# Sums of log decays in four 64x64 tiles, by exchanging the token halves of every second batch

## The chip, the cores and the metric

The kernel runs on one core of a Trainium2 chip. The metric is the device time of one execution, in microseconds. Most single executions of one and the same kernel here lie within about 1% of their median (the farthest, in e10, 1.6% below it, apart from one of 1174.87 us named below), so differences of less than 1% are read from repeated runs or from the trace, not from one time. The state of a one-core run ("fast" or "slow") is told only by its distance from the fastest run of its kernel: a run over 1.5% above it is left out of the ratio. Where that matters (above all in e10) the text says so.

## The reference

Two stages: a recurrence over 768 tokens for 4 batches of 8 heads, with a 40x40 state for each, and a two-layer perceptron on its output.

```python
# r, k, v, w, a, b: (4, 8, 768, 40) float32; w is the decay, between 0.85 and 0.95
for t in range(S):
    y[:, :, t] = einsum('bhd,bhde->bhe', rt, state)
    Sa = einsum('bhde,bhe->bhd', state, at)
    state_decay = state * wt[:, :, None, :] - einsum('bhd,bhe->bhde', Sa, bt)
    state = state_decay + einsum('bhd,bhe->bhde', vt, kt)
x = y.transpose(0, 2, 1, 3).reshape(B * S, H * D)      # 3072 x 320
h = x @ w_in                                           # 320 -> 2048
out = (0.5 * h * (1 + erf(h / sqrt(2)))) @ w_out       # 2048 -> 320
```

## The kernel before

The recurrence is computed in 12 chunks of C = 64 tokens, everything in float32. The kernel keeps two batches on the two halves of the 128 partitions: partition half e holds the 64 tokens of batch 2e+g, and g (0 or 1) is an index along the free dimension. A "pair" in the prediction below is one value of g. P is 128, HP 64, D 40, H 8, G 2, NP 4, DM 320.

Within a chunk, decays multiply up, so their logarithms are summed over the tokens before. That is a matrix product with a triangular mask. The mask `cum_m` is 128x128 and has two triangles on its diagonal and zeros elsewhere, because the two halves are different batches:

```python
def rows_of(src, c, e):
    return src[G * e:G * (e + 1), :, c * C:(c + 1) * C, :].rearrange("g h t d -> t (g h) d")

def fetch(c, n, src, eng, t=None):            # loads of w, b, k: two DMAs for each
    ...
    for e in range(2):
        eng.dma_start(out=t[half(e)].rearrange("p g h d -> p (g h) d")[:, :, :D], in_=rows_of(src, c, e))

def load_VR(c):                               # the load of v by tokens: two DMAs
    VR = turned_in.setdefault(c, {})["VR"] = VR_ring()
    for e in range(2):
        nc.sync.dma_start(out=VR[half(e)].rearrange(...)[:, :, :D], in_=rows_of(v, c, e))

def sums(c):
    logw = raws.pop((c, "w"))
    cum = duo("cum")[:, :, :DM]
    for g in range(G):
        mm(cum[:, g], cum_m, logw[:, g * DM:(g + 1) * DM])          # 128x128, 320 columns
    pt = duo("wT_ps")...
    for n in range(G * NP):                                         # the same sums, transposed
        for x in range(2):
            for e in range(2):
                mm(pt[half(x), e, n], logw[half(e), at:at + HP], cum_m[half(e), half(e)])
    ...                                                             # exponentials: part, wpT, en
```

The other products of the recurrence run in 64x64 or smaller tiles, several at once (in the profile of the kernel before, the 64 records of a QY group, 263 ns each in the mean, fit in a slot of 1.47 us). Apart from the transposes of the state (tn_ps), only these sums use the whole array.

Each chunk also needs the inverse of a triangular 64x64 matrix per head. GpSimd inverts its 32x32 diagonal blocks (tile W). They go to a scratch area in DRAM (`inv`) and come back in another layout (`Tt`). VectorE transposes them (`L`), and TensorE computes the off-diagonal block (products `J`). All DMAs but a few of the last chunk are issued, in order, by one queue, SyncE's. This is the loop, with the calls that the argument touches kept:

```python
for c in range(2, NCH):
    n, n2 = c + 1, c + 2
    corner(c)                     # J: needs L
    make_X(c)
    fill()                        # one piece of the perceptron of an earlier chunk
    load_next(n2)                 # SyncE issues the loads of w, a, b, k, r
    joined(c)
    ...
    make_QY(c)
    outputs(c)
    fill()
    make_A(n)
    load_VR(n2)                   # SyncE issues the load of v
    sums(n2)                      # cum, wT_ps
    turn_state()                  # tn_ps
    ...
    store_inverse(n)              # SyncE: inv <- W, behind the load of v
    fetch_inverse(n)              # SyncE: Tt <- inv, waits for the store
    make_av(n)
    ...
    make_N(n2)                    # SyncE: N to DRAM and back, for GpSimd
    turn_corner(n)                # VectorE: L <- Tt
    ...
```

So the fetch of the inverse for a chunk stands in SyncE's queue behind the load of v for the chunk after it. Dense work of the perceptron (ph and po) fills TensorE's time between the products.

## Time and profile before

| | before |
|---|---|
| median of the first three runs | 758.54 us (758.03 to 761.15) |
| span of the profiled run | 756.8 us |
| TensorE busy | 690.4 us, 91% |
| one chunk in the steady part | 53.05 us, TensorE busy throughout |

The page of the kernel before has a line for the chain that ended last (shares of the span by engine). In the views PE is TensorE, DVE VectorE, ACT ScalarE and POOL GpSimd; SPq is the queue of SyncE that issues DMAs:

```profile
PE 78%; DVE 5%; POOL 5%; issue 5%; SPq 4%; DMA 3%; ACT 1%; POOLq 0%; DVEq 0%; ACTq 0%
```

TensorE carries the chain. The SPq and DMA shares, 7% together, are the ones to compare later. From about 190 us on, TensorE's slices are full, so any slot that leaves TensorE's queue should shorten the span. The prediction below shows these lines.

### The profile page before, as it was taken

The numbers are of one execution on the slowest core, as the hardware profiler recorded it, in microseconds if no ns is written. First come the engines' busy times: TensorE is split into PE (matmuls) and PEld (weight loads), VectorE is DVE, ScalarE is ACT, GpSimd is POOL, SyncE is SP. The second block draws the span as 40 slices with busy tenths as digits, with TensorE's granted clock in tenths as the row PEclk, the third lists the DMA queues.
The fourth block names the chain that finished last, engine by engine and source line by source line (L and its number), as shares of the span: only waits on it lengthen the run. The fifth ranks groups of instructions, "written<-read, shape, count | busy, mean of one in ns | idle before, by whom it ended". The sixth has DMA issues, their size and how long they took to land.

```text
span 756.8 us, 30335 instructions
## 1 busy us (share of the span) xinstructions
PE 690.4 (91%) x13664; PEld 550.9 (73%) x13664; DVE 320.8 (42%) x452; ACT 209.1 (28%) x254; POOL 317.6 (42%) x778
## 2 busy tenths in 40 slices
PE   7456886884999999999999999999999999999997
PEld 4346775652887887887877877878878878778684
DVE  2777438874244345155244353443352552211000
ACT  5124363241232222330341331322223303102020
POOL 3385146850381471570750842833814806500000
PEclk9655798986999999999999999999999999999999
DMA  9797666095763754755845746648547441110100
GB/s 120 131 173 139 120 188 113 20 165 117 134 119 68 144 111 80 135 106 99 145 86 110 133 90 126 125 82 150 106 82 138 102 78 37 34 36 3 31 5 17
DMA packets 302153, 75.68 MB, mean 100 GB/s; under 512 B 290408, under 2 KB 295304, under 8 KB 302024
## 3 DMA queue, kind: packets, MB, share of 16 engines
q1 hardware_dynamic: 301824, 73.58, 51.5%
q8 instruction: 107, 1.75, 1.0%
q14 instruction: 22, 0.18, 0.1%
q10 hardware_dynamic: 200, 0.16, 0.1%
HBM read 59.54 MB, written 10.22 MB: 92 GB/s over the span
## 4 chain that ended last, share of the span: by engine, by line
PE 78%; DVE 5%; POOL 5%; issue 5%; SPq 4%; DMA 3%; ACT 1%; POOLq 0%; DVEq 0%; ACTq 0%
PE po L823 27%; PE ph L815 26%; PE QY L100 5%; PE J L100 2%; PE sap L100 2%; PE cum L100 2%; PE saT_ps L100 2%; PE N_ps L100 2%; PE M_ps L100 2%; DVE W L629 2%; PE av L100 2%; DVE tmp L627 1%; POOL tmp L627 1%; POOL W L629 1%; PE X L100 1%
## 5 line engine op out<-in xcount | busy, mean ns | idle before, releaser
L823 PE MATMUL po<-w_out_sb,gt 128*128 128x320 f32 x768 | 224.5, 445 | 17.4 <-DVE w_out_sb L299 15.5
L815 PE MATMUL ph<-xt,w_in_sb 64*128 64x256 f32 x1920 | 222.8, 385 | 5.9 <-POOL w_in_sb L304 5.5
L815 PEld LDWEIGHTS ph<-xt,w_in_sb 64*128 64x128 f32 x1920 | 183.9, 189 | 30.3 <-POOL w_in_sb L304 6.3
L823 PEld LDWEIGHTS po<-w_out_sb,gt 128*128 128x128 f32 x768 | 143.9, 193 | 80.5 <-DVE w_out_sb L299 21.0
L627 POOL TENSOR_TENSOR tmp<-W,Nb 128x126 f32<-128x126 f32 (+22 forms) x310 | 113.1, 365 | 157.5 <-DMA Nb<-N 133.9
L629 POOL TENSOR_TENSOR W<-W,tmp 128x126 f32<-128x126 f32 (+22 forms) x310 | 118.2, 381 | 24.3
L817 ACT ACTIVATE gt<-ph 128x1024 f32<-128x1024 f32 x48 | 49.2, 1025 | 166.4 <-PE ph L815 166.3
L827 DVE COPY os<-po 128x320 f32<-128x320 f32 x24 | 11.8, 492 | 90.1 <-PE po L823 90.1
L533 DVE TENSOR_TENSOR SM<-M_ps,upper 128x1024 f32<-128x1024 f32 x12 | 14.7, 1224 | 58.8 <-PE M_ps L100 58.8
L694 DVE COPY Tt<-J 32x512 f32<-32x512 f32 x12 | 8.3, 689 | 66.0 <-ACT Tt L694 66.0
L453 POOL TENSOR_TENSOR ks<-k_raw,part 128x640 f32<-128x640 f32 x10 | 21.2, 2123 | 34.6 <-DMA k_raw<-in_k_dram 17.5
L678 ACT COPY Js<-J 128x256 f32<-128x256 f32 x12 | 4.5, 372 | 107.7 <-PE J L100 107.7
L617 POOL MEMSET W<- 128x512 f32 x10 | 5.3, 530 | 68.8 <-DMA inv<-W 68.8
L772 DVE TENSOR_TENSOR xt<-QY,wpT 128x512 f32<-128x512 f32 x24 | 15.5, 686 | 42.2 <-PE QY L100 42.2
L291 ACT ACTIVATE conv<-conv,rebias 128x320 uint32<-128x320 uint32 (+1 forms) x26 | 16.0, 622 | 46.4 <-DVE conv L290 46.4
L817 ACT ACT_TABLE_LOAD x10 | 12.8, 1283 | 42.4 <-PE ph L815 42.4
L533 DVE TENSOR_TENSOR A<-A_ps,upper 128x1024 f32<-128x1024 f32 x12 | 14.7, 1221 | 22.8 <-PE A_ps L100 22.8
L721 DVE COPY SM<-sap 128x640 f32<-128x640 f32 x12 | 9.9, 824 | 30.3 <-PE sap L100 30.1
L533 DVE TENSOR_TENSOR N<-N_ps,upper 128x1024 f32<-128x1024 f32 x12 | 14.7, 1225 | 18.5 <-PE N_ps L100 18.5
L100 PEld LDWEIGHTS QY<-SM,nb 64*64 64x64 f32 x768 | 18.7, 140 | 5.2 <-issue 3.6
L100 PE MATMUL QY<-SM,nb 64*64 64x104 f32 x768 | 21.3, 263 | 1.3 <-DVE SM L533 1.3
L100 PEld LDWEIGHTS av<-VR,A 64*64 64x64 f32 x768 | 13.9, 149 | 11.1 <-DVE A L533 6.3
(159 smaller groups left out, 899.5 us busy)
## 6 DMA issues: line engine op xcount, KB each, us to landing
Nb<-N SPq DMA_DIRECT2D x22, 256.0 KB
VR<-in_v_dram SPq DMA_DIRECT2D x24, 160.0 KB
out_dram<-os SPq DMA_DIRECT2D x48, 80.0 KB
w_tile<-in_w_dram SPq DMA_DIRECT2D x22, 160.0 KB
b_raw<-in_b_dram SPq DMA_DIRECT2D x22, 160.0 KB
k_raw<-in_k_dram SPq DMA_DIRECT2D x22, 160.0 KB
w_out_sb<-in_moe_w_out_dram SPq DMA_DIRECT2D x11, 320.0 KB
N<-N SPq DMA_DIRECT2D x48, 64.0 KB
```

What stands on the lines that cost most here:

```text
L100: nc.tensor.matmul(o, lhsT, rhs, start=first, stop=True, skip_group_check=True)
L291: nc.scalar.activation(power, power, ACT.Relu, bias=rebias, scale=8.0)
L453: eng.tensor_tensor(ks[:, :, :, :D], raws.pop((c, "k")), rwv, ALU.mult)
L533: nc.vector.tensor_tensor(to, pt, upper.unsqueeze(1).to_broadcast([P, 2 * G * NP, C]), ALU.mult)
L627: eng.tensor_tensor(t, W[:, :rows, j:j + 1].to_broadcast([P, rows, rest]), Nb[:, j:j + 1, j + 1:].to_broadcast([P, rows, rest]), ALU.mult)
L629: eng.tensor_tensor(W[:, :rows, j + 1:], W[:, :rows, j + 1:], t, ALU.add)
L721: nc.vector.tensor_copy(SM.rearrange("p g q (a x) c -> p x (g q a) c", x=2)[:, :, :, :D], sap.rearrange("p x g q a d -> p x (g q a) d"))
L772: nc.vector.tensor_tensor(xt[:, :NP, g * P:(g + 1) * P].rearrange("p i (e t) -> p i e t", e=2), Y, wp[:, g, :, :, :C], ALU.mult)
L815: nc.tensor.matmul(ph[:, x, s], w_in_sb[half(x), kt, p * P:(p + 1) * P], xt[half(x), kt], start=kt == 0, stop=kt == NK - 1)
L817: nc.scalar.activation(gt[:, 4 * q:4 * q + 4].rearrange("p (x s) t -> p x s t", x=2), ph, ACT.Gelu)
L823: nc.tensor.matmul(po[:, g], gt[:, f, g * P:(g + 1) * P], w_out_sb[:, f], start=f == 0, stop=f == NF - 1)
L827: nc.vector.tensor_copy(os, po[:, g])
```

## The change

Half of each 128x128 product for the sums is multiplication with zeros. Four products of 64x64 (2 halves by 2 values of g) do the same work without the zeros, but in the old layout all four would fall on the two diagonal tiles of the array (e12 below runs that: a chunk took 52.7 to 52.8 us). The change puts batch 2e+1 on the other half of the partitions (g = 1 exchanged), from chunk 4 on. Then the output of g = 1 goes from half e to half 1-e, and the four products occupy all four tiles (the slot of the sums was 0.54 us, against 1.27 before).

The price: the two values of g of one load now lie on different halves, and the change cuts each load of b, k and v in two by g (w stays whole, since its halves are exchanged by the sums themselves). Two copies out of PSUM are cut in four, because av and sap now put g = 1 in the other bank (no run here tried them without that). TensorE's tile order changes in several products. This is the core of the diff:

```diff
+    def tokens(c, e, g):
+        return half(e ^ g if c >= NB else e)
+    def bank(c, x, g):
+        return x ^ g if c >= NB else x
+    def rows_of_one(src, c, e, g):
+        return src[G * e + g, :, c * C:(c + 1) * C, :].rearrange("h t d -> t h d")
...
     def fetch(c, n, src, eng, t=None):
         for e in range(2):
-            eng.dma_start(out=t[half(e)]..., in_=rows_of(src, c, e))
+            if n == "w" or c < NB:
+                eng.dma_start(out=t[half(e)]..., in_=rows_of(src, c, e))
+                continue
+            for g in range(G):
+                eng.dma_start(out=t[tokens(c, e, g), g], in_=rows_of_one(src, c, e, g))
...                                   # load_VR: cut in the same way
     def sums(c):
-        for g in range(G):
-            mm(cum[:, g], cum_m, logw[:, g * DM:(g + 1) * DM])
+        if c < NB:
+            ...                       # as before
+        else:
+            for g in range(G):
+                for e in range(2):
+                    mm(cum[tokens(c, e, g), g], cum_m[half(e), half(e)], logw[half(e), g * DM:(g + 1) * DM])
...
     def make_av(c):
-            mm(av[half(e ^ x), x, g, i], t["A"][half(e), x, g, i], t["VR"][half(e), g, q, m, :D])
+            mm(av[half(e ^ x), bank(c, x, g), g, i], t["A"][tokens(c, e, g), x, g, i], t["VR"][tokens(c, e, g), g, q, m, :D])
-        nc.scalar.copy(avs[:, :, :DM], av.rearrange("p x g i d -> p x (g i d)"))
+        for g in range(G):            # c >= NB
+            for x in range(2):
+                nc.scalar.copy(avs[:, x, :DM].rearrange("p (g n) -> p g n", g=G)[:, g],
+                               av[:, bank(c, x, g), g].rearrange("p i d -> p (i d)"))
...                                   # make_sa: the same with SM; A, RV, M, QY: other tiles
```

More of the change, by code (lines that the diff above doesn't have):

```diff
@@ L145, in fetch @@
         for e in range(2):
-            eng.dma_start(out=t[half(e)].rearrange("p g h d -> p (g h) d")[:, :, :D], in_=rows_of(src, c, e))
+            if n == "w" or c < NB:
+                eng.dma_start(out=t[half(e)].rearrange("p g h d -> p (g h) d")[:, :, :D], in_=rows_of(src, c, e))
+                continue
+            for g in range(G):
+                eng.dma_start(out=t[tokens(c, e, g), g], in_=rows_of_one(src, c, e, g))
         raws[c, n] = t
@@ L192, in load_VR @@
         for e in range(2):
-            nc.sync.dma_start(out=VR[half(e)].rearrange("p g q m d -> p (g q m) d")[:, :, :D], in_=rows_of(v, c, e))
+            if c < NB:
+                nc.sync.dma_start(out=VR[half(e)].rearrange("p g q m d -> p (g q m) d")[:, :, :D], in_=rows_of(v, c, e))
+                continue
+            for g in range(G):
+                nc.sync.dma_start(out=VR[tokens(c, e, g), g].rearrange("p q m d -> p (q m) d")[:, :, :D],
+                                  in_=rows_of_one(v, c, e, g))
     def load_v(c):
@@ L394, in sums @@
         cum = duo("cum")[:, :, :DM]
-        for g in range(G):
-            mm(cum[:, g], cum_m, logw[:, g * DM:(g + 1) * DM])
+        if c < NB:
+            for g in range(G):
+                mm(cum[:, g], cum_m, logw[:, g * DM:(g + 1) * DM])
+        else:
+            for g in range(G):
+                for e in range(2):
+                    mm(cum[tokens(c, e, g), g], cum_m[half(e), half(e)], logw[half(e), g * DM:(g + 1) * DM])
         pt = duo("wT_ps").rearrange("p e (n t) -> p e n t", t=C)
@@ L533, in masked, with products @@
         nc.vector.tensor_tensor(to, pt, upper.unsqueeze(1).to_broadcast([P, 2 * G * NP, C]), ALU.mult)
-    def products(name, lT, rT, swap):
+    def products(name, lT, rT, swap, c=0):
         pt = duo(name).rearrange("p j (g n t) -> p j g n t", g=G, n=NP)
@@ L541, in products @@
                     for j in range(2):
-                        mm(pt[half(e ^ j if swap else e), j, g, n], lT[half(j, D), g, n, e],
+                        mm(pt[half(e ^ j) if swap else tokens(c, e, g), j, g, n], lT[half(j, D), g, n, e],
                            rT[half(j, D), g, n, e])
@@ L575, in make_RV @@
         t = turned_in[c]
-        t["RV_ps"] = products("RV_ps", t["vT"], t["rT"], False)
+        t["RV_ps"] = products("RV_ps", t["vT"], t["rT"], c >= NB)
         if mask:
@@ L586, in make_A @@
         t["A"] = work.tile([P, 2, G, NP, C], FP32, tag="nT", name="A")
-        t["A_ps"] = products("A_ps", t["kT"], t["aT"], False)
+        t["A_ps"] = products("A_ps", t["kT"], t["aT"], False, c)
         if mask:
@@ L598, in make_av @@
         for g, i, x, e, q, m in units():
-            mm(av[half(e ^ x), x, g, i], t["A"][half(e), x, g, i], t["VR"][half(e), g, q, m, :D])
+            mm(av[half(e ^ x), bank(c, x, g), g, i], t["A"][tokens(c, e, g), x, g, i], t["VR"][tokens(c, e, g), g, q, m, :D])
         avs = t["avs"] = avs_ring()
-        nc.scalar.copy(avs[:, :, :DM], av.rearrange("p x g i d -> p x (g i d)"))
+        if c < NB:
+            nc.scalar.copy(avs[:, :, :DM], av.rearrange("p x g i d -> p x (g i d)"))
+            return
+        for g in range(G):
+            for x in range(2):
+                nc.scalar.copy(avs[:, x, :DM].rearrange("p (g n) -> p g n", g=G)[:, g],
+                               av[:, bank(c, x, g), g].rearrange("p i d -> p (i d)"))
     inverses = {}
@@ L718, in make_sa @@
             at = (g * NP + i) * D
-            mm(sap[half(e), x, g, q, i % NA], Tt[half(e ^ x), x, g, i], xs[half(e ^ x), x, at:at + D])
+            mm(sap[tokens(c, e, g), bank(c, x, g), g, q, i % NA], Tt[half(e ^ x), x, g, i], xs[half(e ^ x), x, at:at + D])
         SM = t["SM"] = SM_ring()
-        nc.vector.tensor_copy(SM.rearrange("p g q (a x) c -> p x (g q a) c", x=2)[:, :, :, :D],
-                              sap.rearrange("p x g q a d -> p x (g q a) d"))
+        to = SM.rearrange("p g q (a x) c -> p x (g q a) c", x=2)[:, :, :, :D]
+        if c < NB:
+            nc.vector.tensor_copy(to, sap.rearrange("p x g q a d -> p x (g q a) d"))
+            return
+        for g in range(G):
+            for x in range(2):
+                nc.vector.tensor_copy(to[:, x, g * NP:(g + 1) * NP],
+                                      sap[:, bank(c, x, g), g].rearrange("p q a d -> p (q a) d"))
     def make_saT(c):
@@ L738, in make_M @@
         t = turned_in[c]
-        masked(flat(t["SM"])[:, :, D:], products("M_ps", t["saT"], t["rT"], False))
+        masked(flat(t["SM"])[:, :, D:], products("M_ps", t["saT"], t["rT"], c >= NB))
     def make_y2(c):
@@ L759, in make_QY @@
             for g, i, x, e, q, m in units():
-                mm(t["QY"][g][half(x), e, i], l_[half(e), g, head_of(i, x)], r_[half(e), g, q, m],
+                mm(t["QY"][g][half(x), e, i], l_[tokens(c, e, g), g, head_of(i, x)], r_[tokens(c, e, g), g, q, m],
                    state[0] is None and n == 0 and i == 0)
```

## The prediction

> **What bounds the kernel now.** I read the page first (busy shares, the 40 slices, the chain), then the busy time of the engines in seven equal stretches, then TensorE's timeline through one chunk, then the waits of TensorE and of the DMA-issuing queue.
>
> From the page, the slices of TensorE and of its granted clock:
>
> ```profile
> PE   7456886884999999999999999999999999999997
> PEclk9655798986999999999999999999999999999999
> ```
>
> The reader is to see two stages. For about a quarter of the span (to about 190 us) TensorE has gaps and the clock varies: loading and converting of the weights and the first chunks. From there on every slice is full and the clock is full. All the changed work lies in the second stage: chunks 4 to 11 are prepared two chunks ahead, by the loop that serves chunks 2 to 9.
>
> The view of stretches, cut at the start of the product that follows the sums in each chunk (columns: length, TensorE busy with instructions, clock, DMA share, GB/s):
>
> ```profile
> 230.68:283.73 53.05, 53.05 (x1134) 1.00 0.60 112
> 283.73:336.78 53.05, 53.05 (x1134) 1.00 0.60 111
> ...
> 548.98:602.03 53.05, 53.05 (x1133) 1.00 0.58 112
> ```
>
> Each chunk takes 53.05 us to the second decimal, and TensorE is busy for all of it. Asked for TensorE's waits between 230 and 654 us, the trace lists none. So here the time is the sum of TensorE's slots: what leaves its queue leaves the span, unless some other engine becomes late.
>
> The timeline of TensorE around the sums of one chunk (start, length, group):
>
> ```profile
> 489.06 4.57 PE L823 MATMUL po<-w_out_sb,gt 128*128 128x320 f32 x16
> 493.57 1.16 PE L100 MATMUL A_ps<-aT,en 40*64 40x64 f32 x64
> 494.66 1.34 PE L100 MATMUL cum<-w_tile,cum_m 128*128 128x320 f32 x4
> 495.93 1.16 PE L100 MATMUL wT_ps<-cum_m,w_tile 64*64 64x64 f32 x64
> 497.02 1.09 PE L418 MATMUL tn_ps<-ident,st 128*128 128x128 f32 x8
> ```
>
> Groups overlap at their edges, so I measure a slot from start to next start. The sums (cum) take 494.66 to 495.93, 1.27 us, on the full 128x128 array, between two groups in 64x64 tiles. The four records are two matmuls, each in two passes for float32.
>
> [...] The group QY<-SM,nb has 64 passes of 64x104 and the slot 1.47 us (486.05 to 487.52); a pass of 320 columns costs 4.5/16 = 281 ns in the po groups, so one of 104 columns some 90 ns, and 64 of them would take 5.8 us one after another: four run at once. And 32-matmul groups of about the same size have a slot of 0.98 us when the next group is in 64x64 too (QY<-rT, 479.50 to 480.49) and 1.07 to 1.10 when it is not (A_ps, N_ps, RV_ps, wT_ps): about 0.1 us for a switch. [...] by these two rows and two others (ScalarE 128x256 372 ns, VectorE 128x320 492 ns):
>
> ```profile
> L721 DVE COPY SM<-sap 128x640 f32<-128x640 f32 x12 | 9.9, 824 | 30.3 <-PE sap L100 30.1
> L601 ACT COPY avs<-av 128x640 f32<-128x640 f32 x12 | 8.3, 691 | 45.9 <-PE av L100 45.9
> ```
>
> Per column that is (691-372)/384 = 0.83 ns on ScalarE and (824-492)/320 = 1.04 ns on VectorE, and about 160 ns fixed on both.
>
> **The change part by part**, for each of eight chunks. The comparison of the instruction order shows nothing else: no group moves, only six groups change their shape or count.
>
> 1. Sums. Two matmuls 128x128 by 320 become four in the four 64x64 tiles: half of the work of the old ones was with the zero blocks of the mask. Each tile has two passes of 320 columns, 2 x 281 = 562 ns, and all four run beside each other with some 15 ns of issue between them (64 records in 0.96 us for sap). Slot about 0.6 us against 1.27: **-0.67 us**.
> 2. No more switch from A_ps into the sums: A_ps's slot of 1.09 should fall towards 1.0: **-0.08 us**. The switch after the sums was part of the 1.27; the one after wT_ps stays.
> 3. Order of tiles. With halves exchanged for the second pair, av and sap visit the tiles as a b c d d c b a, and QY at distances 3 and 5 rather than 4, so a tile is sometimes asked twice running. The group saT_ps has such an order already (a b b a) and its slot (1.13) is only some 0.04 above groups with a regular order. For four groups I take **+0.1 us** in all. RV, M and A only permute tiles in a regular order: 0.
> 4. Copies in four. ScalarE: 4 x (160 + 160 x 0.83) = 1,170 ns for 691, +0.48 us; VectorE: 4 x (160 + 160 x 1.04) = 1,305 for 824, +0.48 us. ScalarE then idles 11.0 us before its next copy, and the sum that reads avs comes 12 us later. VectorE idles 5.6 us before the mask of M_ps, the next thing TensorE needs from it. The buffers of four PSUM slots come round later than that. On the path: 0.
> 5. Loads. Of b, k and v, two DMAs of 64x16x40 become four of 64x8x40: same bytes, same 160-byte rows, six issues more. The same shape took 634 ns an issue in the start (r, four of them); the issues now take about 0.66 us for v. So the queue gets 6 x 0.64 = 3.8 us more per chunk, if nothing is absorbed.
>
> Sum on TensorE: -0.67 - 0.08 + 0.1 = **-0.65 us per chunk, eight times: -5.2 us**, period 52.4 us.
>
> **The rivals.** (a) The DMA-issuing queue becomes the bound. This is the only one I take seriously. Its waits in a chunk:
>
> ```profile
> SPq L651 <- DMA inv<-W: 3.7, 1, 3.7
> SPq L619 <- DMA N<-N: 1.6, 1, 1.6
> SPq L146 <- POOL tmp L627: 0.7, 1, 0.7
> SPq L780 <- DVE st L795: 0.6, 1, 0.6
> SPq L570 <- DVE L L664: 0.5, 1, 0.5
> ```
>
> That is all between 283 and 336 us: the first two are round trips through DRAM on its own path, and only 1.8 us are free. Other chunks have up to 8 us free, about 5 on average. Adding 3.8 us brings the queue close to TensorE's 52.4 us. What is late then is the fetch of the inverse (Tt), which stands behind the added v loads: issued 10.6 to 12.4 us after the sums start, landed some 4 us later, transposed at +16.6, and TensorE needs the result at +19.8 (corner products J). So about 2 us of lateness are free after the shift of 0.65 us. The v loads alone add 1.3 us; those of b and k (2.6) meet a wait of 0 to 3 us on a VectorE transpose[...]. So I expect small stalls in one to three chunks, **+0.4 us in all**; if nothing is absorbed and each chunk loses 1.5 us, the gain is gone (760). (b) The four tiles don't overlap on such wide matmuls, or the two passes block each other: eight passes of 281 ns, 2.2 us, would cost 8 x 1 us and give 766. QY speaks against it at 104 columns. (c) VectorE or ScalarE becomes late: 43% and 28% busy in these chunks, against. (d) Nothing is gained since the sums hide: against, TensorE has no gap that could hide them.
>
> **The range and the chances.** 758.5 - 5.2 + 0.4 gives **753.7 us**. If the sums take 0.8 us and stalls 1.5 us: 757; if the switch saves twice what I took and the tile order costs nothing: 751.8. So 751.8 to 757.2, eight times in ten. A change of 2% is 15 us, three times the whole gain, and neither rival (a) nor (b) reaches it: faster by over 2% 0.01, within 2% 0.975, slower by over 2% 0.015.
>
> **What would show it.** In the changed profile: the slot of cum about 0.6 us, that of A_ps about 1.0; the chunk period 52.4 us with TensorE still busy throughout; slots of sap, av and QY longer by under 0.05 us each; four copies of about 290 and 330 ns with the same next starts; the queue's free waits per chunk reduced by 2 to 4 us. Wrong it would be if TensorE showed waits in J (on the transpose L) in most chunks, if the period changed from chunk to chunk, or if cum's slot stayed above 1 us.

## The result

| | before | changed |
|---|---|---|
| median, runs of the same rounds | 758.28 us (755.59 to 761.15, 6 runs) | 767.11 us (760.32 to 770.52, 6 runs) |
| profiled run: span | 756.8 us | 765.0 us |
| profiled run: mean granted clock of TensorE | 0.936 | 0.926 |

The ratio is 1.0105, with a 95% interval from 1.0059 to 1.0152. Ratios here and below are the mean time of one kernel's fast runs over that of the other's fast runs of the same rounds, so they are not quite the ratio of the medians. The change loses 1%. That is within 2%, but the time lies 10 us above the range of the prediction, on the other side of zero.

**What went as intended.** The timeline of TensorE around the first of the changed sums (start, length, group), changed kernel:

```profile
228.03 1.16 PE L109 MATMUL A_ps<-aT,kT 40*64 40x64 f32 x64
229.01 0.74 PE L109 MATMUL cum<-w_tile,cum_m 64*64 64x320 f32 x8
229.55 1.12 PE L109 MATMUL wT_ps<-cum_m,w_tile 64*64 64x64 f32 x64
230.61 1.09 PE L444 MATMUL tn_ps<-ident,st 128*128 128x128 f32 x8
```

From start to next start, the sums take 229.55 - 229.01 = 0.54 us, against 1.27 before. A_ps takes 0.98 against 1.09, and wT_ps 1.06 against 1.09. Together the three slots shrink by 0.87 us. The groups by form show the cut copies of the changed kernel (busy time, mean ns of one; then idle time before):

```profile
L759 DVE COPY SM<-sap 128x160 f32<-128x160 f32 x32 | 8.1, 317 | 23.5 <-PE sap L109 23.5
L632 ACT COPY avs<-av 128x160 f32<-128x160 f32 x32 | 7.0, 306 | 29.6 <-PE av L109 29.6
```

They cost what was worked out for them (about 326 and 292 ns each), and both engines were idle ahead of them.

**What did not.** The page of the changed kernel: TensorE's granted clock in the 40 slices, and the chain that ended last:

```profile
PEclk9655898985999999999999999998999989999999
...
PE 70%; SPq 7%; POOL 7%; DMA 7%; issue 5%; DVE 2%; ACT 1%; POOLq 0%; DVEq 0%; ACTq 0%
```

In the steady part, where every slice was at 9 before, two slices are down to 8. SPq and DMA carry 14% of the chain instead of 7%. The view of stretches is cut again at the start of wT_ps of each chunk (length, TensorE busy with instructions, clock, DMA share, GB/s):

```profile
229.55:281.73 52.18, 52.18 (x1141) 1.00 0.60 114
...
333.90:386.21 52.31, 52.31 (x1141) 1.00 0.57 108
386.21:441.41 55.20, 53.83 (x1140) 0.97 0.58 111
441.41:493.89 52.48, 52.33 (x1141) 1.00 0.57 106
493.89:552.37 58.48, 55.54 (x1140) 0.94 0.59 113
552.37:604.54 52.17, 52.17 (x1140) 1.00 0.55 103
```

Undisturbed chunks take 52.17 or 52.18 us, so the gain of 0.87 us per chunk is there in full. But two chunks take 55.20 and 58.48 us. In both, TensorE's busy time is shorter than the stretch, so it waited, and the busy time itself is longer than 52.17 at a lower mean clock, so it also worked slowly. The waits of TensorE from 229.5 to 660 us name the place (total, times, longest):

```profile
PE J L109 <- DVE L L696: 7.0, 3, 2.9
```

There are three waits, of 1.37, 2.94 and 2.68 us, the third in the tail after 604.54 us. All are of J for the transpose L. The chain of waits from 493 to 532 us (start, length, what) says what L was waiting for:

```profile
507.18 0.58 SPq L673
507.81 4.18 DMA inv<-W
...
512.42 2.04 DMA Tt<-inv
...
514.55 0.72 DVE L L696
...
515.41 0.77 PE J L109 x49
...
517.73 7.32 PE ph L853 x40
```

SyncE issued the store of the inverse only at 507.18 us (line 673 is `store_inverse`; line 213, just before it in the full chain, is the load of v). The data went out and came back, the transpose took 0.72 us, and J could begin at 515.41 us, although TensorE had been ready from 512.47. Then look at the last line: 40 dense products ph take 7.32 us. In the kernel before, the same 40 take 4.5. The view of stretches around this wait shows why, by its clock column:

```profile
512.47:515.41 2.94, 0.00 (x0) 1.00 0.63 99
515.41:516.50 1.09, 1.09 (x91) 1.00 0.44 89
...
517.50:520.00 2.50, 2.50 (x22) 0.50 0.51 80
...
523.50:524.50 1.00, 1.00 (x14) 1.00 0.89 204
```

About a microsecond after the wait, the granted clock fell to half, and it stayed there for nearly 7 us (until some 523.4). The wait of 2.94 us made its chunk 58.48 - 52.17 = 6.3 us longer. The wait of 1.37 us made its chunk 3.0 us longer in the same way (0.58 and 0.56 in the mean of the four microseconds from 407, so some 3.4 us at half), and after the third wait (2.68 us) the clock was at half for nearly 7 us again.

**Why SyncE is late.** From the timeline of SyncE's queue, summed over the eight chunks and divided by eight, the issues of the three tensors take this long per chunk:

| us per chunk | b | k | v | sum |
|---|---|---|---|---|
| before (two issues each) | 2.41 | 1.60 | 1.41 | 5.42 |
| changed (four issues each) | 3.12 | 3.07 | 3.14 | 9.33 |

The load adds 3.9 us a chunk. An issue of a half load has a median of 633 to 640 ns, and one of a whole load had 672 ns for v: half the bytes take nearly the same time to issue. Less is left of what the queue had free before. Its waits for other engines (all but the two round trips through DRAM) were 4.2 us per chunk on average before, and are 2.4 now. In the stretch from 333.9 to 386.2 us, where they are fewest, almost only the round trips are left:

```profile
SPq L683 <- DMA inv<-W: 2.3, 1, 2.3
SPq L651 <- DMA N<-N: 1.6, 3, 1.0
SPq L162 <- POOL W L661: 0.4, 1, 0.4
```

The decisive table is the moment at which the fetch of the inverse goes out, in microseconds after wT_ps starts, for the eight chunks. A column is named by the chunk whose sums begin the stretch; the inverse fetched in it is that of the chunk before.

| chunk | 4 | 5 | 6 | 7 | 8 | 9 | 10 | 11 |
|---|---|---|---|---|---|---|---|---|
| before | 8.5 | 10.5 | 9.4 | 11.0 | 11.1 | 10.9 | 9.3 | 10.1 |
| changed | 11.7 | 11.9 | 14.1 | 16.5 | 15.4 | 18.2 | 12.8 | 17.9 |
| wait of J, changed | 0 | 0 | 0 | 1.37 | 0 | 2.94 | 0 | 2.68 |

These are the lines of SyncE's timeline from which column 9 is taken (load of v and fetch; wT_ps starts at 495.93 before and at 493.89 in the changed kernel), first before, then changed:

```profile
500.11 1.41 SPq L193 DMA_DIRECT2D VR<-in_v_dram  x2
506.87 1.91 SPq L651 DMA_DIRECT2D Tt<-inv  x4
...
503.97 3.11 SPq L213 DMA_DIRECT2D VR<-in_v_dram  x4
512.04 1.92 SPq L683 DMA_DIRECT2D Tt<-inv  x4
```

TensorE reaches J 18.6 us after that start. The three waits fit a limit near 15.2 us for the fetch: 16.5 - 15.2 = 1.3, 18.2 - 15.2 = 3.0, 17.9 - 15.2 = 2.7. Before, the fetch went out at 8.5 to 11.1 us in every chunk. Now it slips, because the queue needs more than a period of TensorE for its work: from one fetch to the next it took 52.4 to 57.3 us, 54.5 on average, and TensorE needs 52.17. A longer chunk of TensorE then lets it catch up, as after the columns 7 (16.5, then 15.4) and 9 (18.2, then 12.8).

**The account of the profiled runs.** The stretch before 230 us ended 1.13 us earlier in the changed kernel (230.68 against 229.55). Seven undisturbed periods would have gained 7 x 0.87 = 6.1 us. The periods' excesses over 52.18 sum to 0.13 + 3.02 + 0.30 + 6.30 = 9.75 us, and the tail is 5.7 us longer. That makes -1.1 - 6.1 + 9.75 + 5.7 = +8.2 us, which is the difference of the spans. Of the 15.45 us of losses, 7.0 are waits of J. The clock columns give some 3.4, 6.8 and 6.8 us at half clock after the three waits. Half of that time is lost, which makes an estimate of 8.5 us and covers the other 8.5. The small excesses of 0.13 and 0.30 us have no wait with them that the view lists (the second has 0.15 us without an instruction, and the limit of 15.2 us would give 0.2 there).

### The profile page after: what moved, and what is told of

Same layout as the page of the kernel before. It is cut to its first block, busy times and chain, and to the rows that moved or that the text cites. A ratio compares the mean times of both kernels' runs of the same rounds, so it can differ in the third digit from the quotient of the medians.

```text
span 765.0 us, 30525 instructions
## 1 busy us (share of the span) xinstructions
PE 692.0 (90%) x13696; PEld 554.1 (72%) x13696; DVE 321.8 (42%) x476; ACT 210.5 (28%) x278; POOL 321.4 (42%) x778
## 4 chain that ended last, share of the span: by engine, by line
PE 70%; SPq 7%; POOL 7%; DMA 7%; issue 5%; DVE 2%; ACT 1%; POOLq 0%; DVEq 0%; ACTq 0%
PE ph L853 27%; PE po L861 22%; PE QY L109 5%; DMA inv<-W 3%; PE J L109 2%; PE X L109 2%; POOL W L661 1%; POOL tmp L659 1%; PE sap L109 1%; PE saT_ps L109 1%; DMA a_pairs<-in_a_dram 1%; PE A_ps L109 1%; POOL st L661 1%; PE M_ps L109 1%; POOL st L659 1%
## 5 line engine op out<-in xcount | busy, mean ns | idle before, releaser
L853 PE MATMUL ph<-xt,w_in_sb 64*128 64x256 f32 x1920 | 228.7, 392 | 6.2 <-POOL w_in_sb L325 5.8
L853 PEld LDWEIGHTS ph<-xt,w_in_sb 64*128 64x128 f32 x1920 | 188.0, 193 | 32.4 <-POOL w_in_sb L325 6.6
L659 POOL TENSOR_TENSOR tmp<-W,Nb 128x126 f32<-128x126 f32 (+22 forms) x310 | 119.4, 385 | 152.5 <-DMA Nb<-N 128.9
L479 POOL TENSOR_TENSOR ks<-k_raw,part 128x640 f32<-128x640 f32 x10 | 18.0, 1802 | 24.0 <-DMA k_raw<-in_k_dram 17.3
L855 ACT ACT_TABLE_LOAD x10 | 12.8, 1283 | 49.4 <-PE ph L853 49.4
L810 DVE TENSOR_TENSOR xt<-QY,wpT 128x512 f32<-128x512 f32 x24 | 15.4, 683 | 25.0 <-PE QY L109 25.0
L109 PEld LDWEIGHTS av<-VR,A 64*64 64x64 f32 x768 | 13.9, 149 | 10.9 <-DVE A L559 6.1
L109 PEld LDWEIGHTS J<-L,N 32*32 32x32 f32 x768 | 8.6, 112 | 16.7 <-issue 16.7
```

The lines of the kernel that those rows point to most:

```text
L109: nc.tensor.matmul(o, lhsT, rhs, start=first, stop=True, skip_group_check=True)
L479: eng.tensor_tensor(ks[:, :, :, :D], raws.pop((c, "k")), rwv, ALU.mult)
L659: eng.tensor_tensor(t, W[:, :rows, j:j + 1].to_broadcast([P, rows, rest]), Nb[:, j:j + 1, j + 1:].to_broadcast([P, rows, rest]), ALU.mult)
L810: nc.vector.tensor_tensor(xt[:, :NP, g * P:(g + 1) * P].rearrange("p i (e t) -> p i e t", e=2), Y, wp[:, g, :, :, :C], ALU.mult)
L853: nc.tensor.matmul(ph[:, x, s], w_in_sb[half(x), kt, p * P:(p + 1) * P], xt[half(x), kt], start=kt == 0, stop=kt == NK - 1)
L855: nc.scalar.activation(gt[:, 4 * q:4 * q + 4].rearrange("p (x s) t -> p x s t", x=2), ph, ACT.Gelu)
```

## The experiments

My theory after this reading was that the count of DMA issues on SyncE makes the fetch of the inverse late, that TensorE waits for it, and that each such wait is followed by half clock. The rivals: the changed copies or tile orders do it, the smaller transfers themselves are slower, or the half clock has another cause than the wait. In the tables below, medians of the kernel before were 758.17, 758.59, 759.06 and 759.46 us in the four batches of runs. One of its runs in the last batch took 1174.87 us; it was not counted as fast.

### The loads alone, the copies alone

e1_loads_alone is the kernel before with only this edit: the loads of b, k and v from chunk 4 on are cut by g, and nothing is exchanged.

```diff
-            eng.dma_start(out=t[half(e)]..., in_=rows_of(src, c, e))
+            if n == "w" or c < NB: ...   # as before
+            for g in range(G):
+                eng.dma_start(out=t[half(e), g], in_=rows_of_one(src, c, e, g))
...                                   # load_VR: cut in the same way
```

> The kernel before with only the loads of b, k and v of chunks 4 to 11 cut into four DMAs each (six issues more per chunk, no exchange, sums as before). Queue theory (the issuing queue is late, TensorE waits in J for L, and a wait makes its clock halve): TensorE's chunk stays at 53.05 us, which gives the queue 0.9 us more per chunk than in the change, so it is on the edge: 759 to 764 us, with waits of J on L in at least one chunk and the queue's wait on the vT transpose gone. Rival 1 (the copies in four or the order of tiles cost the time): equal to before within 0.3%, no wait in J.

Measured: median 767.3 us (762.6 to 768.75, 4 runs), ratio 1.0101 [1.0045, 1.0157]. That is above the range expected for the queue theory (759 to 764). J waited 4.7 us in three chunks. The stretch of the worst chunk:

```profile
498.17:559.05 60.88, 57.51 (x1133) 0.92 0.58 109
```

The kernel before, slowed by nothing but the cut loads, shows the same picture: 60.88 us for 53.05, part wait and part low clock. Of the 3.4 us in which TensorE stood still there, 2.3 are the wait of J. Another 1.0 is a pause inside the product X just after it, for which the profile names no cause.

e2_copies_alone is the kernel before with only the copies of avs and SM cut in four.

```diff
-        nc.scalar.copy(avs[:, :, :DM], av.rearrange("p x g i d -> p x (g i d)"))
+        for g in range(G):
+            for x in range(2):
+                nc.scalar.copy(avs[:, x, :DM].rearrange("p (g n) -> p g n", g=G)[:, g], av[:, x, g].rearrange("p i d -> p (i d)"))
...                                   # SM: cut in the same way, on VectorE
```

> The kernel before with only the two PSUM copies of chunks 4 to 11 cut into four each. Queue theory: equal to before, 758.3 within 0.3%, chunk period 53.05 us. Rival 1: slower by 4 to 9 us, TensorE waiting for a copy.

Measured: median 758.84 us (20 runs), ratio 1.0003 [0.9981, 1.0026], no wait of J. The copies are free.

### The change without its loads

e15_uncut_wrong is the change with b, k and v loaded whole, as before. It is wrong on purpose (relative error 0.82), since the tokens of g = 1 lie on the wrong half. Its instructions on TensorE, VectorE and ScalarE are those of the change.

```diff
-            if n == "w" or c < NB:
+            if True:                 # in fetch; the same in load_VR
```

> The changed kernel with its loads of b, k and v as in the kernel before (two DMAs each, tokens not exchanged), so its result is wrong on purpose; tiles, order of tiles, banks, cut copies and all else as in the change. Queue theory: the loads are the whole loss, so no wait in J and every chunk at 52.18 us: 758.5 - 7.0 = 751.5 us (750 to 753). If something else in the change costs as well: above 755.

Measured: median 752.6 us (751.98 to 753.29, 4 runs), ratio 0.992 [0.9896, 0.9943], no wait of J. Two of its stretches, at the places of the bad chunks:

```profile
387.86:440.03 52.17, 52.17 (x1141) 1.00 0.62 114
...
492.20:544.37 52.17, 52.17 (x1140) 1.00 0.62 115
```

Everything but the loads gives the whole gain, so the loads are the whole loss. Together with e1 this says more: the loads cost the kernel before 1.01%, and the changed kernel is 1.05% slower than before, although TensorE needs 7 us less in it. Where the queue sets the pace, the time saved on TensorE is worth nothing that these runs can show.

### The count of issues, or the size

e6_tiny and e16_tiny6 are the kernel before with nine and six additional tiny DMAs per chunk, of 64 rows of 16 bytes, into a tile that nobody reads, issued beside the loads of b, k and v.

```diff
+    def extra(src, c, n=3):              # n=2 in e16_tiny6
+        if c < NB:
+            return
+        for _ in range(n):
+            ...
+            nc.sync.dma_start(out=tiny[half(e), at:at + 4], in_=src[0, 0, c * C:(c + 1) * C, :4])
```

> The kernel before with nine tiny DMAs more per chunk (chunks 4 to 11; 64 rows of 16 bytes each, into a tile that nobody reads), three after each of the loads of b, k and v: at some 0.45 us an issue about 4 us more of the issuing queue, with hardly a byte more. Queue theory: as with the cut loads alone, waits of TensorE in J on L in some chunks, 761 to 768 us. Rival 2 (cut loads are slower inside the DMA engines; the number of issues is harmless): equal to before within 0.4%, no wait in J.

Measured: median 785.66 us (4 runs), ratio 1.0349 [1.0321, 1.0377]; J waited 14.1 us in seven chunks. A tiny issue has a median of 594 to 596 ns, where some 0.45 us had been expected (what a load of r by pairs takes in the kernel before, 450 ns), and the loss is far above the expected range (761 to 768).

> The kernel before with six tiny DMAs more per chunk (64 rows of 16 bytes), two after each of the loads of b, k and v. If the count of issues alone is the cause, as much as the cut loads alone: 767 us within 4, three or so waits in J of 1 to 3 us. If the size of the cut transfers matters besides: clearly less, 758 to 762. Nine of them gave 785.7.

Measured: median 766.03 us (764.03 to 767.71, 4 runs), ratio 1.0095 [1.0065, 1.0126]. In its profile J waited once (some three times were expected), and the stretch with that wait of 2.9 us was 6.1 us too long:

```profile
390.84:449.99 59.15, 56.28 (x1133) 0.94 0.60 110
```

Six more issues of 1 KB cost as much as the six that came from cutting loads in two (1.0095 against 1.0101). So the number of issues is enough to explain the loss, whatever they carry. From six to nine the loss grows more than three times (0.95% to 3.49%), so it is a limit that is crossed and no fixed price per issue.

### What a wait costs

e8_stall is the kernel before with the transpose L repeated 4 to 10 times in chunks 4 to 10, so that J waits a known time. It was run once, so its state is unknown; only its own stretches are compared.

```diff
-        nc.vector.transpose(L, flat(inverses[c][0])[:, :, :BL])
+        for _ in range({4: 4, 5: 5, 6: 6, 7: 7, 8: 8, 9: 9, 10: 10}.get(c, 1)):
+            nc.vector.transpose(L, flat(inverses[c][0])[:, :, :BL])
```

> The kernel before with the transpose of L, on which J waits, repeated 4, 5, 6, 7, 8, 9 and 10 times on VectorE for chunks 4 to 10 (0.63 us each): a wait of TensorE in J of known and growing size, with the DMAs untouched. Clock theory (a wait over some 1 to 1.5 us lets the clock be granted at half for about 7 us afterwards): the chunk's period grows by the wait itself for waits below about 1 us, and by the wait plus 2 to 3.5 us above, with a stretch of granted clock 0.5 after each such wait. Rival (a wait costs itself): the period grows by the wait and nothing else, clock 1.00 throughout.

Measured: waits of 0.54, 1.28, 2.03, 2.78, 3.53 and 4.27 us. The stretches of three of the chunks:

```profile
389.45:443.85 54.40, 53.12 (x1134) 1.00 0.60 109
443.85:498.99 55.14, 53.11 (x1134) 1.00 0.61 109
498.99:559.70 60.71, 55.74 (x1134) 0.94 0.52 98
```

Waits up to 2.03 us cost themselves (55.14 - 53.05 = 2.09) at full clock. The stretch with the wait of 2.78 us was 7.66 us longer, with the clock at 0.94 in the mean. Not all of that is the wait and the clock, for TensorE's waits in this stretch are two:

```profile
PE J L100 <- DVE L L665: 2.8, 1, 2.8
PE X L100 <- issue: 2.2, 1, 2.2
```

The second is a pause inside X, which began some 1.8 us after J did and for which the profile names no cause. The next wait, of 3.53 us, had no such pause, and its stretch was 59.02 - 53.05 = 5.97 us longer, again at 0.94. A wait alone, with the loads untouched, therefore brought the half clock here. The limit is not a fixed length, though: 2.03 us was harmless here (the theory had expected the loss from 1 to 1.5 us on), 2.8 us was harmless in a stretch of e4 below, and 1.37 us was enough in the changed kernel. In the windows cut around the waits of the changed kernel the clock is at 1.00 or at 0.50, with values between where a window holds the change (0.78 and 0.81 in windows of one microsecond). The half clock lasted some 3.4 us after the wait of 1.37 us, and some 6.8 us after each of those of 2.94 and 2.68 us. What decides whether a wait brings it, no run here tells.

### Taking the issues off the path

Four attempts to relieve SyncE while keeping the change.

e4_act_queue is the change with the g = 1 halves of b, k and v issued from ScalarE's queue.

```diff
-            for g in range(G):
+            for g in ((0,) if eng is nc.sync else (1,)):
...
-                nc.sync.dma_start(out=VR[tokens(c, e, g), g]...
+                (nc.scalar if g else nc.sync).dma_start(out=VR[tokens(c, e, g), g]...
...
+            for name, src in (("b", b), ("k", k)):
+                fetch(n2, name, src, nc.scalar, raws[n2, name])
```

> The changed kernel with half of the cut loads (the second pair of b, k and v) issued from ScalarE's queue, so that the first queue has as many issues as before; bytes, shapes and number of DMAs as in the change. Queue theory: no wait in J, all chunk periods 52.18 us, so 758.3 - 8 x 0.87 = 751.3 us (750 to 753). Rival 2 (the DMA engines are slower with the smaller transfers, whoever issues them): waits in J on L remain, 762 to 768.

Measured: a miss. Median 765.41 us (20 runs, of which 5 counted as slow), ratio 1.0065 [1.0036, 1.0094]; J waited 9.8 us in six chunks. Its longest wait, 2.8 us, left the clock full:

```profile
229.75:285.58 55.83, 52.56 (x1141) 1.00 0.61 112
```

The waits of SyncE from 230 to 655 us have a kind that was not there before:

```profile
SPq L177 <- DMA VR<-in_v_dram: 13.5, 13, 3.1
```

Line 177 issues the loads of r and of v by pairs, into other tiles than VR. In the same list the loads of b and k (line 162) waited 13.1 us, in 13 waits, for the loads of a. The changed kernel's list has neither kind. So with half of the cut loads on ScalarE's queue, SyncE has 26.6 us of new waits for loads into tiles that the waiting issue doesn't touch, 3.3 us per chunk over eight chunks. What makes it wait there, the trace does not show. The experiment did not test what it was made for.

e7_out_act is the change with the outputs stored from ScalarE's queue, which takes four issues per chunk off SyncE.

```diff
-                        nc.sync.dma_start(out=out[row:row + C], in_=os[half(e)])
+                        (nc.scalar if c >= 2 else nc.sync).dma_start(out=out[row:row + C], in_=os[half(e)])
```

> The changed kernel with the four stores of the outputs of each chunk issued from ScalarE's queue, idle at that time; all loads stay cut and stay where they are. Queue theory: 2.3 us less for the first queue, net 1.5 us more than before, less than the least slack of before: waits in J gone or under 1 us in all, 750 to 754 us. Rival 2: the loads are as slow as in the change, 763 to 768.

Measured: a miss, and the worst of all: median 864.07 us (5 runs), ratio 1.1389 [1.1369, 1.1409]. J waited 84.5 us in seven chunks, and SyncE waited for those stores. In its waits over the whole run the longest entry is of the issues of xt (line 818):

```profile
SPq L818 <- DMA out_dram<-os: 95.7, 6, 16.8
```

The changed kernel, which issues these stores from SyncE, has no such wait from 230 to 655 us. As in e4, issues of SyncE waited for DMAs of data that they don't touch. That this is what delayed J in every chunk is argued and not shown.

e10_vr_behind is the change with the load of v moved behind the fetch of the inverse in SyncE's order.

```diff
-            load_VR(n2)              # ahead of sums(n2)
             ...
             fetch_inverse(n)
             make_av(n)
+            if more2:
+                load_VR(n2)
```

> The changed kernel with the four loads of v moved in the issuing queue from ahead of the inverse's store and fetch to behind them; the same issues in number and shape. Queue theory in the form 'what is late is the fetch of the inverse': the fetch goes out some 2.8 us earlier, waits in J gone or rare, 751 to 756. If the queue's pace itself (all issues of a chunk longer than 52.2 us) is the bound, its lateness grows from chunk to chunk and waits come back in the last chunks: 756 to 763. Rival 2: as the change, 763 to 768.

Measured: median 757.53 us (745.44 to 762.16, 20 runs). The ratio of fast runs is 0.9936 [0.9907, 0.9965], but one run at 745.44 us made 12 of the 20 count as slow, and the mean of all 20 is only 0.16% under that of the kernel before. I take it as no clear gain. Its profile is of one of the runs that counted as slow; at 760.1 us and a clock of 0.939 it is usable for the order of events. J waited 0.7 us in all. The lateness had moved, as the waits of VectorE from 228 to 660 us show:

```profile
DVE aT L185 <- DMA a_pairs<-in_a_dram: 34.2, 6, 7.9
```

The fetch of the inverse was in time, and the loads behind it came late instead, up to 7.9 us for a. Moving one item forward in this full queue moved the wait to another item.

e14_before_out is the control for merged output stores: the kernel before, with the two output DMAs per g made one. e11_wswap_out and e13_after_out_vr combine the same merge with other edits, to free two issues per chunk.

```diff
-                    for e in range(2):
-                        row = (G * e + g) * S + c * C
-                        nc.sync.dma_start(out=out[row:row + C], in_=os[half(e)])
+                    row = g * S + c * C
+                    to = out.rearrange("(e s) d -> e s d", e=2)[:, row:row + C]
+                    nc.sync.dma_start(out=to, in_=os)
```

> Control: the kernel before with the outputs in one DMA per token group. TensorE is the bound and nothing waits for the queue there: equal to before within 0.3%, chunk period 53.05 us. If it is faster by more, part of the gain of the kernels with this edit is not the sums.

> The changed kernel with the outputs in one DMA per token group (net four issues more than before instead of six) and the loads of v behind the fetch of the inverse. Queue theory with the queue's pace as the bound: 1.3 us less per chunk than with the loads of v moved alone; waits of VectorE on a and r, and those of TensorE in cum and tn, shrink to a third or less; 751 to 755 us. If the pace is not it: 757.5 as with the loads of v moved alone.

> The kernel with w alone exchanged, and each chunk's outputs stored by one DMA per token group instead of two (two issues less per chunk): as many issues as the kernel before. Queue theory: no wait in J longer than 1 us, every chunk at 52.18 us, 758.4 - 8 x 0.87 = 751.4 us (749.5 to 752.5), no slower than with w alone exchanged (752.6). If the single wait of 1.9 us there was not the queue's count but chance: equal to 752.6.

Measured: e14 771.5 us (4 runs), ratio 1.0137 [1.0089, 1.0185]. e13 (the change, merged outputs, v behind the fetch) 785.93 us (4 runs), 1.035 [1.0323, 1.0378]. e11 (e5 below with merged outputs) 773.51 us (6 runs), 1.019 [1.0162, 1.0217]. All three are misses, and e14 shows that the merge itself does harm (J waited 4.2 us in it, with the loads untouched). In e14's view of the output tensor, who waited for its stores (us, times):

```profile
  DVE os L827: 39.4, 10
```

VectorE waited 39.4 us for the buffer os to be stored; the kernel before has no such wait. e11 has the same wait, 38.3 us in 10 times. An issue of a merged store took 586 ns in the median, against 594 ns for one of the two before, so the issue itself took no longer. Why the merged stores held the buffer, these runs do not show.

### Keeping the gain with fewer issues

e5_w_swap exchanges only w, instead of b, k and v: w is cut by g (two issues more per chunk instead of six), the sums run in four tiles with their output in the plain order, and the exponentials of the transposed sums are cut in three where they read the exchanged halves. No product, copy or other load changes.

```diff
-            eng.dma_start(out=t[half(e)]..., in_=rows_of(src, c, e))
+            if n != "w" or c < NB: ...   # as before
+            for g in range(G):
+                eng.dma_start(out=t[half(e ^ g), g], in_=rows_of_one(src, c, e, g))
...
+            for e in range(2):
+                mm(cum[half(e), g], cum_m[half(e ^ g), half(e ^ g)], logw[half(e ^ g), g * DM:(g + 1) * DM])
...
+            nc.scalar.activation(to[:, :, :NP], pt[:, :, :NP], ACT.Exp, scale=scale)
+            for e in range(2):
+                nc.scalar.activation(to[:, e, NP:], pt[:, 1 - e, NP:], ACT.Exp, scale=scale)
```

> The kernel before with w alone loaded in exchanged halves (two issues more per chunk rather than six), the sums in four 64x64 tiles with their output in the plain order, and the two exponentials of the turned decays cut into three each; no token of b, k, v is exchanged, no copy is cut. Queue theory: 1.3 us more of the queue per chunk, below the least slack seen before (1.8 us), so no or hardly any wait in J and the full gain of TensorE: 751.3 us (750.5 to 754). If two issues are enough to make it late: 755 to 760 with waits in J. If ScalarE's four extra starts (0.16 us each) are on the path: a wait of TensorE for nT or av in each chunk, 753 to 757.

Measured: **752.6 us** (746.81 to 758.74, 20 runs), ratio 0.9926 [0.9902, 0.9951], correct. One run counted as slow. Undisturbed periods are 52.17 to 52.18 us, as here:

```profile
490.21:542.39 52.18, 52.18 (x1141) 1.00 0.59 112
```

The issues of w, b, k and v take 8.7 us per chunk, against 7.1 before. In its profile one wait of J was left, 1.9 us, in the tail. This version beats both kernels, by more than any other correct one tried.

e12_diag is the kernel before with the four products on the two diagonal tiles: no exchange, no load changed. It splits the gain into the part from the tiling mode and the part from running four at once.

```diff
-            mm(cum[:, g], cum_m, logw[:, g * DM:(g + 1) * DM])
+            for e in range(2):           # c >= NB
+                mm(cum[half(e), g], cum_m[half(e), half(e)], logw[half(e), g * DM:(g + 1) * DM])
```

> The kernel before with the sums of chunks 4 to 11 in 64x64 tiles on the diagonal only: four matmuls of 64x320, two in each of two tiles; nothing exchanged, no DMA changed. It has the saved switches of the tiling mode without the four-fold overlap. If overlap is the larger part: each tile has four passes of some 270 ns, slot of cum 1.08 to 1.12 us for 1.27, that of A_ps 0.98 for 1.09; chunk period 52.7 to 52.8 us, 755.5 to 756.5 us. If the saved switch were most of the gain: slot near 0.6, period near 52.2.

Measured: 756.27 us (753.73 to 759.07, 8 runs), ratio 0.9952 [0.9934, 0.9971]. The period is 52.7 to 52.8 us. Of the 0.87 us per chunk, some 0.33 come with two tiles in one tiling mode and no DMA at all, and 0.54 come from the other two tiles working beside them. The 0.33 are not the saved switches alone: in e12's timeline the first passes of wT_ps start before the last of cum (at 496.59 us, the last of cum at 496.85), so the two groups overlap as well.

e17_wswap_j and e18_after_j are e5 and the change with J moved behind X and one dense piece, so that the fetch has some 5.6 us longer.

```diff
-        corner(c)
         make_X(c)
         fill()
+        corner(c)
+        fill()
...
-        fill()                        # one dense piece less further on
```

> The kernel before with w alone exchanged (two issues more) and the corner products J moved behind X and one piece of the dense layer (a piece is taken from ahead of av and put between J and J2), so L may come 5.6 us later. Queue theory with bounded lateness: no wait in J, 52.18 us per chunk, 751.3 us (749.5 to 753). If moving the piece makes TensorE wait for nT, av or a PSUM buffer: 753 to 760.

> The changed kernel with J moved in the same way. If the lateness is bounded at some 5 us: no waits, 751.5 us. If the queue's pace is the bound (about 1 us per chunk more than TensorE's 52.18): waits in J gone but lateness moving to the loads of a and r and from there to VectorE, as with the loads of v moved, 755 to 760.

Measured: 775.76 us (4 runs), ratio 1.0219 [1.0179, 1.0259], and 775.78 us (4 runs), ratio 1.0224 [1.0161, 1.0287]. No wait of J was left in either. That bounds nothing for the changed kernel, since the stretches of e18 took 54.4 to 56.7 us and so left its queue 2.3 to 4.5 us more than 52.17. My move made a new wait, in e17 from 190 to 800 us:

```profile
PE ph L836 <- ACT gt L838: 14.7, 9, 1.8
```

Two dense pieces followed each other closely, and the second waited for the Gelu of the first, up to 1.8 us in each chunk. In two of seven stretches of e17 and in four of e18 the mean clock was 0.97 as well; in the others it stayed full. Both are misses by an edit of mine and say nothing for or against the theory. A better place for J was not looked for.

## Why the prediction was wrong

It forecast 753.7 us and held 751.8 to 757.2 for the range. The class (within 2%) was right, the sign and the range were wrong.

- **The bound of the kernel** was read rightly: the time is the sum of TensorE's slots unless another engine becomes late. e15 gives 752.6 us once nothing is late.
- **Step 1, the sums**: -0.67 us forecast, -0.73 measured (1.27 to 0.54). Rival (b), no overlap of wide tiles, is refuted by that slot and by e12.
- **Step 2, the switch**: -0.08 forecast for A_ps, -0.11 measured, and another -0.03 at wT_ps that was not forecast.
- **Step 3, the order of tiles**: +0.1 us forecast, nothing measured (the slots of sap 0.96, av 0.95 and QY 1.48 us stayed as they were). The sum on TensorE came to -0.87 instead of -0.65 us per chunk.
- **Step 4, the copies**: right in size (317 and 306 ns each) and in effect (e2: none). The 160 ns fixed in each are an estimate from four rows of the trace (691 and 372 ns on ScalarE, 824 and 492 ns on VectorE).
- **Step 5, the loads**: six issues, +3.8 us forecast, +3.9 measured. The hope that part of it would be absorbed held for b, which grew by 0.71 us (2.41 to 3.12), and not for k and v (1.47 and 1.73).
- **Rival (a), the step that failed**: "So I expect small stalls in one to three chunks, +0.4 us in all". The place (the fetch of the inverse behind the loads of v, the wait of J for L) was right, and the number of stalls (three) was right in the profiled run. The size was 15.45 us in the profiled run instead of 0.4. The worst case that it allowed, each chunk losing 1.5 us, was given as 760. Its own numbers make 758.5 - 5.2 + 8 x 1.5 = 765.3, close to what was measured. Three things were wrong in the term. First, it set an average of 5 us of free queue time against 3.8 us more. The waits that it had read were 5.8, 1.8, 7.9, 2.6, 2.9, 5.1 and 3.5 us in the seven chunks, 4.2 on average, and in four of the seven less than the 3.8 us to be added. Free time of one chunk can't be saved up for a later one, while lateness is carried on: the fetch slipped from 11.7 to 16.5 us in four chunks. Second, it took a wait at its own length. The trace shows half clock after the waits, and the waits of 7.0 us stand in losses of 15.45. Third, it kept the 5.2 us of gain and added the stall to it. Once the queue sets the pace, a faster TensorE only reaches the wait sooner (e1 and the change lose the same 1%). One reading erred the other way: the fetch could be 15.2 - 11.1 = 4.1 us later than in the latest chunk of before, where the prediction saw about 2. (Its offsets of 10.6 to 12.4 us leave out the first of these chunks, with 9.7.)
- **The signs to look for** named a period that changes from chunk to chunk and waits of J. Both appeared, in three of eight chunks rather than in most.

The upper end of the range has a small slip as well: with sums of 0.8 us and stalls of 1.5 us the terms give 756.4, where 757 was written.

What stays open: the exact condition of the half clock (1.37 us brought it once, 2.8 us in e4 did not), what the pauses in X are that stand beside it in e1 and e8, what makes SyncE's issues wait in e4 and e7 for DMAs of data that they don't touch, and whether the two would gain without those waits.

## What to carry to other kernels

Cutting a DMA in two cost a whole issue more on its queue here, 633 to 640 ns (median) for 80 KB, and an issue of 1 KB took hardly less, 594 to 596 ns. Before adding issues, add up that queue's time per period, its own round trips included, and compare it with the period, rather than with an average of its idle time. Where the clock fell after a wait of TensorE, the wait cost about twice its length in these runs (6.3 us for 2.94, 3.0 for 1.37, 6.1 for 2.9, 5.97 for 3.53): reckon with that where it may fall. Exchange the tensor with the fewest issues and consumers: one here (w) gave the gain that three gave away.
